# S4 convolution and MLP on one core: the outer products of the small tables as four operations, and a new order for everything ahead of the MLP

## The chip, the cores and the metric

The kernel runs on one core of one Trainium2 chip. Its time is device microseconds from one launch, and the median of three runs stands for it. The five engines are named as the profile names them: PE multiplies matrices, DVE and ACT do element-wise work, POOL is GpSimd, SP issues transfers. POOL issues transfers too. Each engine takes its instructions strictly in the order in which the program lists them, so an instruction that waits holds up everything behind it on its engine.

## What is computed

One layer with 2048 samples of 512 channels: a state-space convolution (S4) and an MLP, each behind two layer norms in a row. Cut to what matters:

```python
def _A_ref(u, A_re, A_im, B_re, B_im, C_re, C_im, log_dt, Dskip):
    dt = jnp.exp(log_dt)[:, None]
    logdA = dt * (A_re + 1j * A_im)                  # [D=512, N=128]
    P = jnp.exp(logdA[:, :, None] * l[None, None, :])  # l = 0..2047
    K = jnp.einsum("dn,dnl,dn->dl", Cc, P, dt * Bc).real
    y = irfft(rfft(pad(u)) * rfft(pad(K)))[:L]       # long convolution
    return y + u * Dskip
def _B_ref(x, w1, b1, w2, b2):
    h = _gelu(jnp.einsum("bsd,df->bsf", _layernorm(x), w1) + b1)   # F=1376
    return jnp.einsum("bsf,fd->bsd", h, w2) + b2
h  = x + _A_ref(_layernorm(x), ...)
h2 = h + _B_ref(_layernorm(h), ...)
```

## The kernel before

The work runs in two parts: a front, in which the convolution is made, and the MLP (`mlp`), which follows it. The channels are taken in two halves of 256.

**What the front does, stage by stage.** `params` turns the six parameter arrays into angles and logarithms of magnitudes, each split into pieces of bfloat16 that are then transposed by DMA (`TL`, `PL`, `QL`). `norm_in` makes the statistics of the input norm from `x`, some on ACT (`by_act`), the others on DVE (`bn_stats`), and ends in `roots`. `tables` makes the matrices of the Fourier transform (`M`, `Mn`, and turned `R`, `Rn`), partly from spread rows `Dp`. `outer` makes four small tables by outer products, `EP`, `EQ`, `RP` and `RQ`, which are the right-hand sides of later matmuls. `exps` then makes the magnitudes of powers of the state (PE into `ev`, ACT exponentials into `Pt` and `Q`); `p_half` and `q_half` make their phases (PE into `pv` and `qv`, ACT sines into `s` and `sq`, DVE products into `Pt` and `Q`). `kgen` multiplies the two (1024 small matmuls into `kps`, 128 to a step, four steps to each half of the channels) to the samples of the convolution kernel, the "second half's samples" being those of channels 256 to 511. They go to DRAM (`KD_near`, `KD_far`) and come back rearranged as `kt`. The normed input goes through PE (`aps`, `a`) to DRAM (`A_dram`) and comes back as `X`.

`conv` works one half of the channels at a time, in eight blocks `k2`: a spectrum of the kernel samples (`kfps`, 20 matmuls), its evacuation as `kf` (in the second half a real part on DVE, where the constant `tf` is added, and an imaginary part on ACT or DVE), a complex product with the spectrum of the input (`pa`, `pb` on DVE), the way back (`zps`, `z`), and the turn through DRAM (`Zd`, `ZT`). `x_stage` makes the spectrum of the input (`xps`, 8 matmuls per block). `early_rows` and `first_rows` make the first rows `y` for the MLP.

**How the order is made.** Each step is recorded as an operation with `S.op(engine, cost, ...)` and its dependencies. A step with a tuple of engines may stand on either. Nothing is decided while the kernel runs: the list `ORDER` holds one number per step, twice the step's index, plus one for the second engine of the tuple, and `Sched.run` emits the steps in that order. Buffers that rotate are handed out in that order too: three in PSUM with the tag "p", shared by `ev`, `aps`, `pv`, `qv`, `kps`, `xps`, `kfps` and the tables. An order across engines is kept by semaphores.

**Names that the change and the prediction touch.** The outer products stand in `outer`, as two operations on POOL, `make_e` and `make`, and `K.o_oute` and `K.o_out` are what `exps`, `p_half` and `q_half` wait for. Inner broadcasts make them:

```python
def wide(out, w, k, d):
    g.tensor_tensor(..., bc(w.unsqueeze(2), [P, k, d]), bc(m[...].unsqueeze(1), [P, k, d]), ALU.mult)
```

Bulk loads inside the front are the halves of the first MLP weight (`load_w1`, 384 KB each, `w`) and two blocks of the residual input (`residual`, 512 KB each, `X<-in_A_u_dram`). `put` and `get` in `kgen` are the transfers of the kernel samples.

Of the kernel before, what the change touches and what calls it, by code (L numbers as in the profile page):

```python
# [11 lines left out]
ALU = mybir.AluOpType  # L12
# [4 lines left out]
P = 128  # L17
# [14 lines left out]
AT = {"log": 1, "m0": 3, "m1": 3, "bases": 3, "sin0": 3, "exp": (1, 1), "sin": (3, 3)}  # L32
SETS = {1: "natural_log_exp_and_others", 3: "trig_and_small"}
ORDER = [
# [22 lines left out]
]  # L57


# [22 lines left out]
def bc(ap, shape):  # L82
    return ap.to_broadcast(shape)
# [199 lines left out]
def outer(nc, S, K, pp, c2):  # L283
# [7 lines left out]
    m, we = flat[:, 640:704], flat[:, 704:756]  # L291
    wp, wq = (flat[:, a:b].rearrange("p (i c) -> p i c", c=2) for a, b in ((768, 800), (800, 840)))
    g = nc.gpsimd
# [19 lines left out]
            count(nc, wq[p0:p1, at:at + cnt], base, pattern + [[0, 2]])  # L313
    pl = S.at(12.3)

    def wide(out, w, k, d):
        g.tensor_tensor(out[:].rearrange("p i c d -> p (i c) d") if len(out.shape) == 4 else out, bc(w.unsqueeze(2), [P, k, d]), bc(m[:, 0:32].unsqueeze(1) if d == 32 else m[:, 32:48].unsqueeze(1), [P, k, d]), ALU.mult)

    def make_e():
        g.tensor_tensor(m, K.ident[:, 0:64], K.ident[:, 64:128], ALU.add)  # L320
        g.tensor_tensor(m[:, 0:32], m[:, 0:32], m[:, 32:64], ALU.add)
        wide(K.EP, we[:, 0:32], 32, 32)
        wide(K.EQ[:, 0:20], we[:, 32:52], 20, 32)

    def make():
        g.tensor_tensor(m[:, 32:48], m[:, 0:16], m[:, 16:32], ALU.add)
        wide(K.RP, wp.rearrange("p i c -> p (i c)"), 32, 32)
        wide(K.RQ, wq.rearrange("p i c -> p (i c)"), 40, 16)

    K.o_oute = S.op("POOL", 4.0, make_e, [pl])  # L330
    K.o_out = S.op("POOL", 3.6, make, [K.o_oute])


def first_stage(nc, S, K, cp, c2, psp, dram):
# [330 lines left out]
def exps(nc, S, K, big, psp, hh, gate):  # L665
# [7 lines left out]
    for out, w, n, grp in ((K.o_pe, K.EP, 32, "pe"), (K.o_qe, K.EQ, 20, "qe")):  # L673
        S.group = f"{grp}{hh}"
        for b in range(8):
# [10 lines left out]
                o = K.Pt if grp == "pe" else K.Q  # L686
                nc.scalar.activation(o[:, :, 1, dq], cell["v"][:, 0:32 * n].rearrange("p (k d) -> p k d", d=32), ACT.Exp)  # L687

            x = S.op("PE", 0.45, ex, [K.o_tl[2 * hh + b // 4], K.o_oute, K.o_get], acq="p")
            K.o_ex[grp].append(x)  # L690
            out.append(S.op("ACT", 0.95, amp, [x, K.o_get], rel=[x], fun=AT["exp"][hh]))

# [34 lines left out]
def q_half(nc, S, K, sc, psp, hh):  # L727
    K.o_q, K.o_qp = [[], []], [[], []]
    for qd in range(2):
        S.group = f"q{hh}"  # L730
        for g in range(5):
            cell = {}
            b = 16 * hh + 8 * qd
# [16 lines left out]
                tt(nc, o, cell["s"][:], bc(o[:, :, 1:2, :], [P, m1 - m0, 2, nd]), ALU.mult)  # L750

            qe = K.o_qe[4 * qd + g:4 * qd + g + 1] if g < 4 else K.o_qe[4 * qd:4 * qd + 4]
            x = S.op("PE", 0.9, ph, K.o_ql[hh][2 * qd:2 * qd + 2] + [K.o_out] + qe, acq="p")
            K.o_qp[qd].append(x)
            z = S.op("ACT", 0.94, sn, [x], acq="s", rel=[x], fun=AT["sin"][hh])
            K.o_q[qd].append(S.op("DVE", 0.63, mul, [z] + qe, rel=[z]))
# [593 lines left out]
def kernel(ctx, tc, A_u, A_A_re, A_A_im, A_B_re, A_B_im, A_C_re, A_C_im, A_log_dt, A_Dskip,  # L1350
# [64 lines left out]
    part("x0", x_stage, psp, 0)  # L1415
    part("x1", x_stage, psp, 1)
    part("exps1", exps, big, psp, 1, K.o_kgen)
    done = None
    for n, ends in zip((3, 4, 5, 0, 1, 2), held + [K.o_ex["pe"], K.o_ex["qe"], K.o_ex["pe"] + K.o_ex["qe"]]):
# [79 lines left out]
```

## Time and profile before

| | us |
|---|---|
| three runs | 277.79, 280.06, 280.11 |
| median | 280.06 |
| the profiled execution, its own time | 279.49 |
| its span in the trace | 277.7 |
| PE busy | 246.3 (89%) |
| DVE busy | 208.4 (75%) |
| ACT busy | 170.7 (61%) |
| POOL busy | 51.4 (18%) |

The span leaves 1.79 us of that execution's time outside it. A stage table of the trace has one row per stretch of time: its start and end, its length, then busy microseconds and number of instructions of PE, of PE's weight loads, of DVE, ACT and POOL, then the granted clock of PE as a share of full speed, the mean busy share of the DMA engines, and the GB/s that they moved. A row of the timeline has the start, the duration, the engine, the line, the operation, what it wrote and read, its shape, how many instructions are merged in it, and in brackets the idle time of the engine before it and what ended that time. Stretches used here: up to 9.7 us loads and parameters, to 45 the statistics and tables, to 80 the first half's samples, to 97 the second half's exponentials, to 138 the second half's phases and samples together with the first half's convolution, to 152.6 the wait for the second half's samples, filled with other matmuls, to 189 the second half's convolution, and then the MLP.

### The profile page before, as it was taken

Reading aid. Unit: us, or ns where it says so; the run is one execution under the profiler, and the core shown is the slowest. Engines: PE = TensorE matmul, PEld = TensorE weight load, DVE = VectorE, ACT = ScalarE, POOL = GpSimd, SP = SyncE. Lnnn points to the kernel's source line nnn. Section 1 sums busy time; section 2 is a strip of 40 time slices with the busy share of each in tenths; the row PEclk is TensorE's granted clock in tenths of the full one; section 3 lists DMA queues with packets and bytes.
Section 4 is the critical chain, followed back from the end, with each engine's and each line's share of the span. In section 5 each row is a group of like instructions: output and inputs, shape, how many; then the busy total and the mean of one; then the engine's idle time right before and its main releaser. Section 6 shows DMA issues by size and latency. Waiting matters only on the chain.

```text
span 277.7 us, 6118 instructions
## 1 busy us (share of the span) xinstructions
PE 246.3 (89%) x2421; PEld 156.0 (56%) x2421; DVE 208.4 (75%) x447; ACT 170.7 (61%) x244; POOL 51.4 (18%) x121
## 2 busy tenths in 40 slices
PE   3647988788988899999799999889999999999995
PEld 2412333235743467888688887777874544544443
DVE  5799999999897577989588869878992883772012
ACT  5679999999769987683117346446880540630710
POOL 9992001950013300000033430201000000000000
PEclk9855559999977999999979999999999999999999
DMA  5700125997866269700449567767934104114001
GB/s 171 265 0 2 39 56 82 208 258 154 110 194 170 83 205 298 235 2 5 118 105 230 160 185 234 223 196 231 277 80 107 47 17 96 40 24 109 21 21 57
DMA packets 56737, 35.52 MB, mean 128 GB/s; under 512 B 29162, under 2 KB 55156, under 8 KB 56452
## 3 DMA queue, kind: packets, MB, share of 16 engines
q1 hardware_dynamic: 54884, 30.61, 42.7%
q0 software_dynamic: 1824, 4.51, 6.3%
q8 instruction: 19, 0.31, 0.4%
q14 instruction: 10, 0.08, 0.1%
HBM read 18.65 MB, written 11.21 MB: 108 GB/s over the span
## 4 chain that ended last, share of the span: by engine, by line
PE 57%; DVE 30%; ACT 6%; issue 4%; DMA 2%; SPq 1%; DVEq 0%; ACTq 0%
PE o2ps L1299 13%; PE h1ps L1287 12%; PE kfps L996 8%; PE kps L772 5%; DVE pa L79 3%; DVE Pt L79 3%; DVE a L91 3%; PE y L1104 2%; DVE w L79 2%; DVE st L851 2%; DVE w L121 2%; PE ev L683 2%; DVE Q L79 2%; PE aps L867 1%; DVE pb L79 1%
## 5 line engine op out<-in xcount | busy, mean ns | idle before, releaser
L1289 ACT ACTIVATE hT<-h1ps,b_sb 128x512 bf16<-128x512 f32 (+3 forms) x55 | 31.9, 611 | 36.8 <-PE h1ps L1287 36.8
L1287 PE MATMUL h1ps<-y2T,w 128*128 128x512 bf16 (+3 forms) x220 | 40.2, 336 | 0.5 <-DVE y2T L91 0.5
L1299 PE MATMUL o2ps<-w_sb,hT 128*128 128x512 bf16 (+3 forms) x187 | 38.7, 366 | 0.0
L996 PE MATMUL kfps<-kt,M 128*128 128x256 bf16 x320 | 38.6, 273 | 0.0
L79 DVE TENSOR_TENSOR ot<-o2ps,h 128x512 bf16<-128x512 f32 (+1 forms) x17 | 11.1, 659 | 31.3 <-PE o2ps L1299 19.8
L996 PEld LDWEIGHTS <-M 128*128 128x128 bf16 x320 | 31.5, 98 | 5.1 <-issue 0.9
L1287 PEld LDWEIGHTS <-w 128*128 128x128 bf16 (+1 forms) x220 | 21.9, 100 | 15.2 <-issue 0.6
L1299 PEld LDWEIGHTS <-hT 128*128 128x128 bf16 (+1 forms) x187 | 18.2, 98 | 19.7
L127 ACT ACTIVATE sq<-qv 128x1024 bf16<-128x1024 int16 x20 | 19.9, 1042 | 2.3 <-PE qv L742 2.0
L772 PEld LDWEIGHTS <-Pt 128*32 128x32 bf16 x1024 | 18.0, 169 | 5.9 <-issue 3.5
L772 PE MATMUL kps<-Q,Pt 128*32 128x20 bf16 x1024 | 19.0, 221 | 2.5 <-issue 2.0
L79 DVE TENSOR_TENSOR Pt<-s,Pt 128x1024 bf16<-128x1024 bf16 x32 | 20.5, 690 | 0.7 <-ACT s L127 0.7
L89 ACT CAST kf<-kfps 128x512 bf16<-128x512 f32 (+2 forms) x13 | 9.5, 739 | 14.4 <-DVE kf L79 9.3
L127 ACT ACTIVATE s<-pv 128x1024 bf16<-128x1024 int16 x16 | 15.9, 1027 | 2.8 <-issue 1.4
L687 ACT ACTIVATE Pt<-ev 128x1024 bf16<-128x1024 f32 x16 | 15.8, 1025 | 1.5 <-PE ev L683 1.3
L470 POOL DMA_DIRECT2D Dp<-Dd x24 | 12.2, 514 | 22.9 <-DVE u L862 21.8
L91 DVE CAST a<-aps 128x1024 bf16<-128x1024 f32 x11 | 13.4, 1223 | 2.3 <-PE aps L867 2.3
L683 PEld LDWEIGHTS <-TL 128*128 128x128 bf16 x64 | 7.1, 117 | 13.6 <-issue 10.3
L79 DVE TENSOR_TENSOR Q<-sq,Q 128x1024 bf16<-128x1024 bf16 x20 | 13.4, 689 | 0.7 <-ACT sq L127 0.6
L801 POOL DMA_DIRECT2D KD_far<-far x2 | 1.6, 797 | 64.5 <-DVE far L121 64.5
L89 ACT CAST X<-xps 128x1024 bf16<-128x1024 f32 x9 | 8.8, 1019 | 6.9 <-PE xps L908 6.9
L79 DVE TENSOR_TENSOR pa<-pa,pb 128x512 bf16<-128x512 bf16 (+1 forms) x34 | 12.4, 406 | 0.6
(247 smaller groups left out, 508.7 us busy)
## 6 DMA issues: line engine op xcount, KB each, us to landing
A_dram<-a SPq DMA_DIRECT2D x16, 256.0 KB, 3.3
X<-A_dram SPq DMA_DIRECT2D x4, 1024.0 KB, 6.5
Zd<-z SPq DMA_DIRECT2D x14, 256.0 KB, 2.6
ZT<-Zd SPq DMA_DIRECT2D x9, 256.0 KB, 4.2
x<-in_A_u_dram SPq DMA_DIRECT2D x4, 512.0 KB, 7.5
X<-in_A_u_dram SPq DMA_DIRECT2D x4, 512.0 KB, 9.5
out_dram<-ot SPq DMA_DIRECT2D x15, 128.0 KB, 1.7
ZT<-Zd POOLq DMA_DIRECT2D x7, 256.0 KB, 4.1
```

Source lines behind the costliest of these rows:

```text
L79: nc.vector.tensor_tensor(out, a, b, op)
L89: nc.scalar.copy(out, in_)
L91: nc.vector.tensor_copy(out, in_)
L127: nc.scalar.activation(out, v.bitcast(i16)[..., 0:2 * n:2], ACT.Sin, scale=S2PI / 65536)
L470: nc.gpsimd.dma_start(t[o::128 // cnt], bass.AP(row.tensor, row.offset + 1024 * kh, [[0, cnt], [1, 1024]]))
L683: nc.tensor.matmul(v[:, 32 * k:32 * k1], lhsT=K.TL[hh][:, b, :], rhs=w[:, k:k1].rearrange("p k d -> p (k d)"), start=True, stop=True)
L687: nc.scalar.activation(o[:, :, 1, dq], cell["v"][:, 0:32 * n].rearrange("p (k d) -> p k d", d=32), ACT.Exp)
L772: nc.tensor.matmul(kps[32 * g:32 * g + 32, i // 8, at:at + 20], lhsT=Pt[:, :, u, c], rhs=Q[:, :, u, c], start=True, stop=True, tile_positi ...
L996: nc.tensor.matmul(at, lhsT=K.M[:, t, 2 * k2 + k, c, :], rhs=kt[:, t, :], start=(c == 1 or hh == 1) and t == 0, stop=(t == 4))
L1287: nc.tensor.matmul(pt[:fs, 0:n], lhsT=K.w1_sb[:, dc, fc * P:fc * P + fs], rhs=y2T[tb][:, dc, js, :].rearrange("p a b -> p (a b)"), start=( ...
L1289: nc.scalar.activation(hT[tb % 2][:fs, fc, cols], pt[:fs, 0:n], ACT.Gelu_apprx_tanh, bias=K.b1_sb[:fs, fc:fc + 1], scale=1.0)
L1299: nc.tensor.matmul(pt[:], lhsT=h[:fs, fc, jj * P:(jj + 1) * P], rhs=K.w2_sb[:fs, fc, d], start=(fc == 0), stop=(fc == NFC - 1))
```

## The change

`outer` no longer has two operations but five: one for the small mask, on POOL, and one each for `EP`, `EQ`, `RP` and `RQ`, which may stand on DVE or POOL. What waited for both tables of a pair now waits for its own: `exps` for `EP` or `EQ`, `p_half` for `RP`, `q_half` for `RQ`. `ORDER` is a new list of all 711 steps. It puts `RP` on DVE, right behind `roots`, and the three other tables on POOL.

```diff
-    def make_e():
-        g.tensor_tensor(m, K.ident[:, 0:64], K.ident[:, 64:128], ALU.add)
-        ...
-        wide(K.EP, we[:, 0:32], 32, 32)
-        wide(K.EQ[:, 0:20], we[:, 32:52], 20, 32)
-    def make():
-        ...
-        wide(K.RP, wp.rearrange("p i c -> p (i c)"), 32, 32)
-        wide(K.RQ, wq.rearrange("p i c -> p (i c)"), 40, 16)
-    K.o_oute = S.op("POOL", 4.0, make_e, [pl])
-    K.o_out = S.op("POOL", 3.6, make, [K.o_oute])
+    def times(e, out, a, b, op):
+        (g if e == "POOL" else nc.vector).tensor_tensor(out, a, b, op)
+    ...
+    either = ("DVE", "POOL")
+    o_mask = S.op("POOL", 0.8, lambda: mask("POOL"), [pl])
+    K.o_oute = [S.op(either, (1.2, 1.9), lambda e: wide(e, K.EP, ...), [o_mask]),
+                S.op(either, (0.8, 1.2), lambda e: wide(e, K.EQ[:, 0:20], ...), [o_mask])]
+    K.o_out = S.op(either, (1.2, 1.9), lambda e: wide(e, K.RP, ...), [o_mask])
+    K.o_outq = S.op(either, (0.8, 1.2), lambda e: wide(e, K.RQ, ...), [o_mask])
@@ exps
-            x = S.op("PE", 0.45, ex, [K.o_tl[2 * hh + b // 4], K.o_oute, K.o_get], acq="p")
+            x = S.op("PE", 0.45, ex, [K.o_tl[2 * hh + b // 4], K.o_oute[grp == "qe"], K.o_get], acq="p")
@@ q_half
-            x = S.op("PE", 0.9, ph, K.o_ql[hh][2 * qd:2 * qd + 2] + [K.o_out] + qe, acq="p")
+            x = S.op("PE", 0.9, ph, K.o_ql[hh][2 * qd:2 * qd + 2] + [K.o_outq] + qe, acq="p")
@@ ORDER
-    368, 60, 66, 0, 86, 2, 54, 364, ...
+    60, 204, 68, 0, 64, 72, 74, 66, ...
```

What the new list does, read out of it step by step:

- ACT's first sine (`wb`) stands behind the first table of sines, so the first table load of sines at the start falls away; the front has six table loads, not seven.
- On DVE, `freq` (`nf`, `nn`) stands right behind the first product of the parameters; the lower piece of that product stands later. `RP` stands behind `roots`, `last_row` after the first evacuation of `aps`.
- On PE, `cim` is turned ahead of `bre`.
- The scaling of `M` block 1 stands on ACT. Of the evacuations of `aps`, `xps`, `zps` and `kfps` about as many go from DVE to ACT as the other way.
- Ahead of the last `kgen` matmuls of the second half PE has four more blocks (three `xps`, one `zps`) and one `kfps` less; DVE has one more product of the first half (`k2` = 7) ahead of the end of `kgen`. Before the first `kfps` of the second half PE has one more `xps` and one more `zps`.
- The imaginary parts of blocks `k2` = 0 and 5 of the second half stand on DVE.
- Both residual blocks are issued by POOL, behind the last `get` of the second half's samples on POOL; before, the first was issued by SP ahead of the second half's puts. The first half of the weight `w` goes to SP, behind the put of `KD_far` and ahead of three of the five gets; the second to POOL, behind the one get there. The put of `KD_far` goes from POOL to SP and stands behind the first get there, which waits for `KD_near`.
- The bias load of the MLP on POOL stands behind the first half's gets.

More of the change, by code (lines that the diff above doesn't have):

```diff
@@ L314, in outer, with wide, mask @@
     pl = S.at(12.3)
-    def wide(out, w, k, d):
-        g.tensor_tensor(out[:].rearrange("p i c d -> p (i c) d") if len(out.shape) == 4 else out, bc(w.unsqueeze(2), [P, k, d]), bc(m[:, 0:32].unsqueeze(1) if d == 32 else m[:, 32:48].unsqueeze(1), [P, k, d]), ALU.mult)
-    def make_e():
-        g.tensor_tensor(m, K.ident[:, 0:64], K.ident[:, 64:128], ALU.add)
-        g.tensor_tensor(m[:, 0:32], m[:, 0:32], m[:, 32:64], ALU.add)
-        wide(K.EP, we[:, 0:32], 32, 32)
-        wide(K.EQ[:, 0:20], we[:, 32:52], 20, 32)
-    def make():
-        g.tensor_tensor(m[:, 32:48], m[:, 0:16], m[:, 16:32], ALU.add)
-        wide(K.RP, wp.rearrange("p i c -> p (i c)"), 32, 32)
-        wide(K.RQ, wq.rearrange("p i c -> p (i c)"), 40, 16)
-    K.o_oute = S.op("POOL", 4.0, make_e, [pl])
-    K.o_out = S.op("POOL", 3.6, make, [K.o_oute])
+    def times(e, out, a, b, op):
+        (g if e == "POOL" else nc.vector).tensor_tensor(out, a, b, op)
+    def wide(e, out, w, k, d):
+        times(e, out[:].rearrange("p i c d -> p (i c) d") if len(out.shape) == 4 else out, bc(w.unsqueeze(2), [P, k, d]), bc(m[:, 0:32].unsqueeze(1) if d == 32 else m[:, 32:48].unsqueeze(1), [P, k, d]), ALU.mult)
+    def mask(e):
+        times(e, m, K.ident[:, 0:64], K.ident[:, 64:128], ALU.add)
+        times(e, m[:, 0:32], m[:, 0:32], m[:, 32:64], ALU.add)
+        times(e, m[:, 32:48], m[:, 0:16], m[:, 16:32], ALU.add)
+    either = ("DVE", "POOL")
+    o_mask = S.op("POOL", 0.8, lambda: mask("POOL"), [pl])
+    K.o_oute = [S.op(either, (1.2, 1.9), lambda e: wide(e, K.EP, we[:, 0:32], 32, 32), [o_mask]),
+                S.op(either, (0.8, 1.2), lambda e: wide(e, K.EQ[:, 0:20], we[:, 32:52], 20, 32), [o_mask])]
+    K.o_out = S.op(either, (1.2, 1.9), lambda e: wide(e, K.RP, wp.rearrange("p i c -> p (i c)"), 32, 32), [o_mask])
+    K.o_outq = S.op(either, (0.8, 1.2), lambda e: wide(e, K.RQ, wq.rearrange("p i c -> p (i c)"), 40, 16), [o_mask])
 def first_stage(nc, S, K, cp, c2, psp, dram):
```

44 rows, old and new, of the table ORDER are left out of this document.

## Prediction

> **What bounds the kernel now.** I read the stage table first, because the mean shares of the page mix stages with different limits.
>
> ```profile
> 9.70:45.00 35.30, 26.33 (x77) 9.23 (x78) 34.20 (x81) 32.77 (x59) 12.26 (x22) 0.56 0.25 54
> 45.00:80.00 35.00, 29.27 (x605) 16.62 (x604) 33.57 (x61) 31.41 (x36) 12.17 (x24) 1.00 0.86 177
> 80.00:97.00 17.00, 14.24 (x60) 6.02 (x58) 12.05 (x18) 15.55 (x20) 5.41 (x8) 0.80 0.49 134
> 97.00:138.00 41.00, 38.87 (x756) 31.73 (x754) 34.14 (x55) 24.33 (x27) 0.00 (x0) 1.00 0.52 146
> 138.00:152.60 14.60, 14.60 (x120) 12.38 (x119) 11.98 (x17) 6.50 (x8) 4.50 (x7) 0.88 0.66 158
> 152.60:189.00 36.40, 33.60 (x304) 29.39 (x302) 30.00 (x60) 17.11 (x22) 7.14 (x8) 1.00 0.71 204
> 189.00:277.70 88.70, 84.75 (x487) 46.91 (x485) 48.01 (x136) 37.84 (x69) 1.17 (x3) 1.00 0.31 83
> ```
>
> Up to 80 us DVE is the bound (34.20 of 35.30, 33.57 of 35.00), with ACT close behind. From 80 to 97 it is ACT (15.55 of 17.00). From 97 on it is PE: 38.87 of 41.00, then no idle at all, then 33.60 of 36.40. The last 88.7 us are the MLP, whose code the change leaves alone; it only starts earlier or later. So moving work between engines pays up to 80 us only if DVE gets less of it, and after 97 only where PE idles or runs slowly.
>
> The timeline of DVE and POOL shows what POOL's outer products do to DVE.
>
> ```profile
> 9.66 1.29 DVE L79 TENSOR_TENSOR w<-tps_bre,w 128x512 f32<-128x512 f32 x2 [1.83 <-ACT w L89]
> 10.98 0.69 DVE L79 TENSOR_TENSOR w<-w,w 128x512 f32<-128x512 f32 x1
> 12.66 1.90 POOL L317 TENSOR_TENSOR EP<-EQ 128x1024 bf16<-128x1024 bf16 x1
> 12.90 2.21 DVE L79 TENSOR_TENSOR w<-w,w 128x512 f32<-128x512 f32 x1
> 16.37 1.89 POOL L317 TENSOR_TENSOR RP<-EQ 128x1024 bf16<-128x1024 bf16 x1
> 16.77 2.04 DVE L121 SCALAR_TENSOR_TENSOR w<-w,w 128x512 f32<-128x512 f32 x1
> 20.59 0.67 DVE L121 SCALAR_TENSOR_TENSOR w<-w 128x512 f32<-128x512 f32 x1
> ```
>
> The same DVE product takes 0.69 us alone and 2.21 us beside `EP`; the one beside `RP` takes 2.04 us where 0.67 us is its price later. Each time DVE ends about 0.55 us after POOL: one waits for the other.
>
> **The change part by part.** *The outer products and the front (to 80 us).* `RP` leaves POOL, so one lock falls away: 2.04 - 0.67 = 1.37 us of DVE. The other three stay and go on holding DVE. `RP` itself comes to DVE behind `roots`, where DVE has no idle time to hide it. No row shows it on DVE.
>
> ```profile
> L79 DVE TENSOR_TENSOR Pt<-s,Pt 128x1024 bf16<-128x1024 bf16 x32 | 20.5, 690 | 0.7 <-ACT s L127 0.7
> 27.61 0.50 DVE L79 TENSOR_TENSOR nf<-lf,fs 128x336 f32<-128x336 f32 x1
> 28.14 0.58 DVE L73 TENSOR_SCALAR nn<-nf 128x336 int32<-128x336 f32 x2
> 28.75 0.51 DVE L73 TENSOR_SCALAR nn<-nn 128x672 int32<-128x672 int32 x1
> 7.16 0.67 DVE L79 TENSOR_TENSOR M<-w,M 128x512 bf16<-128x512 f32 x1
> 159.25 0.69 DVE L79 TENSOR_TENSOR kf<-kfps,tf 128x512 bf16<-128x512 f32 x1 [1.14 <-ACT kf L89]
> ```
>
> A product of the same size takes 0.69 us, the lower bound; POOL's 1.89 us is the upper. The row most like it is `nf`, which also broadcasts along the innermost axis: 0.50 x 1024 / 336 = 1.52 us with its fixed part counted three times, so I take 1.3. `freq` (`nf` and `nn`, 0.50 + 0.58 + 0.51 = 1.6 us) moves into the 1.83 us in which DVE waits before 9.66, and the 0.67 us piece comes out of cover: -0.9 us. DVE's own sum is then 1.3 - 1.4 - 0.9 = -1.0 us. Against it stand new waits: seven times in the front a DVE step needs an ACT step that needs a DVE step (the first cast of `psi`, its second piece, the cast of `psw`, the logarithm's cast, the arctangent, its piece, the sine for `dirichlet`), and the new lists stand closer together at several of them. A crossing left uncovered costs 1.14 us on the row that shows one alone (159.25, from the second half's convolution). Followed through both lists, the arctangent, the second `psi` piece and half the first cast come out late, so I take +1.6 and the front as +0.6 us; bounds -1.0 (all covered) and +7.6 (seven at 1.14, `RP` at 1.89). One table load less at the start hides nothing: its successor waits for parameters that land at about the same time. `cim` ahead of `bre` only makes room for `freq`.
>
> *The second half's exponentials (80 to 97).* DVE loses the scaling of `M` there and the `aps` that hold PSUM buffers stand later among the exponentials.
>
> ```profile
> 83.27 1.02 ACT L687 ACTIVATE Pt<-ev 128x1024 bf16<-128x1024 f32 x1 [0.88 <-PE ev L683]
> 87.45 2.85 ACT L687 ACTIVATE Pt<-ev 128x1024 bf16<-128x1024 f32 x3 [0.44 <-PE ev L683]
> ```
>
> ACT, the bound, idles 0.88 + 0.44 = 1.32 us here for PE. The new order starts with four short exponentials behind a single `aps`. I take -1.0 us, bounds 0 and -1.32. The scaling of `M`, now on ACT, stands among the `kps` of the first half, where ACT waits for PE; without that cover its 2048 elements cost twice the 1.02 us of a 1024-element row.
>
> *The residual load ahead of the second half's samples.*
>
> ```profile
> 131.78 0.45 SPq L1196 DMA_DIRECT2D X<-in_A_u_dram  x1
> 133.81 2.02 PE L772 MATMUL kps<-Q,Pt 128*32 128x20 bf16 x109
> 137.50 0.45 PE L772 MATMUL kps<-Q,Pt 128*32 128x20 bf16 x15 [1.67 <-issue]
> 138.40:141.30 2.90, 2.90 (x16) 2.01 (x14) 1.97 (x4) 0.36 (x1) 0.79 (x1) 0.50 0.23 75
> 143.99 0.11 PE xps L906
> q1 hardware_dynamic: 281, 0.14, 48.5%
> q8 instruction: 1, 0.02, 5.6%
> ```
>
> In the midst of its last `kps` block PE stands still for 1.67 us, waiting for nothing that the profile names. The transfer queues between 135 and 136 us (last two rows) hold the end of the residual load, issued at 131.78, and one packet of instructions. That PE's instructions queued behind the load is my reading, not a row. From 138.4 to 141.3 the granted clock is 0.50, so that stretch lost 2.90 x 0.5 = 1.45 us; at full clock an `xps` matmul takes 0.11 us. The new order issues this load from POOL behind the `get`s. I take both as gone: -1.67 and -1.45 us, each with 0 as its other bound. [...]
>
> PE's work before the end of `kgen` grows by four blocks of 8 matmuls and shrinks by 20 matmuls, at 0.11 us: (32 - 20) x 0.11 = 1.3 us later; 16 more stand between there and the second half's first `kfps`, and those 20. All of it leaves later stretches that PE bounds too, so it cancels.
>
> *The second half's convolution (152.6 to 189).*
>
> ```profile
> 152.56 4.53 PE L996 MATMUL kfps<-kt,M 128*128 128x256 bf16 x40
> 157.43 0.68 DVE L79 TENSOR_TENSOR kf<-kfps,tf 128x512 bf16<-128x512 f32 x1
> 159.86 0.68 DVE L79 TENSOR_TENSOR pa<-X,kf 128x1024 bf16<-128x1024 bf16 x1
> 160.46 0.69 DVE L79 TENSOR_TENSOR pb<-X,kf 128x1024 bf16<-128x1024 bf16 x1
> 161.18 0.76 DVE L79 TENSOR_TENSOR pa<-pa,pb 128x512 bf16<-128x512 bf16 x2
> 166.65 0.69 DVE L79 TENSOR_TENSOR kf<-kfps,tf 128x512 bf16<-128x512 f32 x1 [2.11 <-ACT kf L89]
> ```
>
> PE has the first block by about 154.8 (half of 4.53 us in), but DVE, still at products of the first half, takes it up at 157.43, and the first product of the second half starts at 159.86. Later DVE waits 1.14 us (159.25) and 2.11 us for ACT's imaginary parts. PE stands 36.40 - 33.60 = 2.80 us in all. The change puts one first-half product (159.86 to 161.85, 2.0 us) ahead of the end of `kgen`, and the imaginary part of the first block on DVE, which ends the crossing there. The backlog then fits into the wait for the samples and PE becomes the bound from the first block. I take -2.0 us of the 2.80; bounds 0 and -2.8.
>
> *The sum.* The profiled execution took 279.49 us, 0.57 below the median of 280.06: 279.49 + 0.6 - 1.0 - 1.67 - 1.45 - 2.0 = 273.97, so 274.0 us.
>
> **The rivals.** *The stall stays.* The blocks of `kgen` stand as close as before (one `zps` between the last two), and instruction packets may run short without any load beside them. For: the load's packets end in the row of 135 to 136 us, the stall only at 137.5. Against: the other three blocks of that half, issued before this load moved data, show no such gap. 274.0 + 1.67 + 1.45 = 277.1 us.
>
> *The second half's samples come back late.*
>
> ```profile
> 139.18 0.33 SPq L803 DMA_DIRECT2D KD_near<-near  x1
> 139.77 0.79 POOL L801 DMA_DIRECT2D KD_far<-far  x1 [42.77 <-DVE far L121]
> 140.89 0.36 SPq L809 DMA_DIRECT2D kt<-KD_near  x1
> 142.62 0.78 POOL L809 DMA_DIRECT2D kt<-KD_far  x1 [2.06 <-DMA KD_far<-far]
> w<-in_B_w_dram POOLq DMA_DIRECT2D x1, 384.0 KB, 7.3
> ```
>
> The put of `KD_far` now stands on SP behind a `get` that waits for `KD_near`, 140.89 - 139.18 = 1.7 us after its put: it starts 2.1 us after the near put instead of 0.6. Behind it on SP come two small transfers and half of `w`, then three of the five `get`s, for which every `kfps` of that half waits. `w` would start at about 3.3 and land at 10.6 us after the near put; the `get`s, if they land only behind it with 2.85 us of their own (what far's put took, 139.77 to 142.62) and a second such for the queue, at 16.3. PE needs them at 152.6 - 139.2 = 13.4, less 1.45 for the restored clock, plus 0.4 for what moves into the gap ((20 + 16 - 32) x 0.11): 12.4. That is 3.9 us of waiting, 277.9 us. Against it: transfers of this size overlapped in this stretch before.
>
> *The front slips (slower).* DVE takes its steps in order, so each ACT step that comes late stops it, and ACT then starts its 16 exponentials late too. Place: 18 to 46 us. Price: at the upper bound +7.6 in place of +0.6: 281.0 us. It decides from the sixth uncovered crossing (0.6 + 6.1 us over the forecast). For: DVE and ACT were both nearly without idle there, and POOL's three locks stay. Against: both lists keep distance at four of seven.
>
> **How the numbers follow.** Forecast 0.50; the stall stays 0.14; late samples 0.16; the front slips 0.20. All gains in full give 279.49 - 1.0 - 1.32 - 1.67 - 1.45 - 2.8 = 271.25, the low end at 271.0; the high end is the slip, 281.0. A measurement here can tell about 1% from no change: under 277.3 and over 282.9 us. Faster takes the forecast and 0.05 of the staying stall, 0.55; slower takes 0.15 of the slip (its crossings can cost more than 1.14) and 0.03 of the late samples, 0.18; the rest, 0.27, lies within.
>
> **What would show it.** Right: no DVE product near 2 us beside `RP`, which takes 1.3 us on DVE around 45; the first half's samples done at about 80 as before; no gap in the last `kps` and a clock near 1.0 behind it; the first second-half product within 4 us of its first `kfps`; PE idle under 1 us to the MLP. Wrong: DVE gaps behind ACT between 18 and 46, or a `kfps` released by a `kt` transfer.

## The result and the profile after

| | before | after |
|---|---|---|
| median of 20 runs each | 280.1 us (276.16 to 281.9) | 275.9 us (273.64 to 279.68) |
| ratio after/before | | 0.9888, 95% interval 0.9858 to 0.9918 |

The changed kernel is 1.1% faster; 274.0 us was forecast. Measured twice more, beside the experiments, its ratio was 0.9816 (0.9766 to 0.9866) and 0.9772 (0.9707 to 0.9837). A ratio leaves disturbed runs out on both sides (in the group of `after_res`, 12 of the 17 runs of the kernel before), so it need not be the ratio of the medians beside it.

The profile read here is that of a second measurement (`after_again`): 272.38 us for that execution, span 270.6 us. In the first one, of 278.16 us, PE's clock was at half in three places between 46 us and the MLP, here in none; the last section comes back to this. Three rows of the stage table after, in the columns of the one before:

```profile
80.00:97.00 17.00, 14.39 (x81) 7.40 (x83) 12.46 (x19) 16.73 (x22) 5.55 (x10) 1.00 0.82 182
138.00:152.60 14.60, 14.60 (x136) 13.08 (x135) 11.71 (x20) 6.16 (x7) 6.58 (x10) 1.00 0.96 244
152.60:189.00 36.40, 32.85 (x297) 28.30 (x295) 29.36 (x66) 19.64 (x30) 7.51 (x10) 1.00 0.72 199
```

Two things strike the eye: the clock of 138 to 152.6 went from 0.88 to 1.00, and in that same stretch the transfer engines are now busy 0.96 of the time, where it was 0.66. A table by fixed times mixes stages that have moved, so I went on by milestones: rows that both kernels have, at the end of each stage. First before, then after; the table loads of ACT open the first half's sines, the second half's exponentials and its sines, `near` ends `kgen`, the `kf` is the first real part of the second half, and `st<-y` is the first statistic of a whole row.

```profile
49.59 1.28 ACT L161 ACT_TABLE_LOAD   x1
80.07 1.28 ACT L161 ACT_TABLE_LOAD   x1
95.56 1.28 ACT L161 ACT_TABLE_LOAD   x1
138.80 0.35 DVE L121 SCALAR_TENSOR_TENSOR near<-kps,half_sign,ku 128x128 bf16<-128x128 f32 x1 [2.73 <-ACT ku L776]
190.96 0.76 DVE L1254 BATCH_NORM_STATS2 st<-y 128x6 f32<-128x256 f32 x2 [0.84 <-PE y L1151]
```

```profile
47.73 1.28 ACT L161 ACT_TABLE_LOAD   x1
78.06 1.28 ACT L161 ACT_TABLE_LOAD   x1
92.07 1.28 ACT L161 ACT_TABLE_LOAD   x1
133.97 0.35 DVE L121 SCALAR_TENSOR_TENSOR near<-kps,half_sign,ku 128x128 bf16<-128x128 f32 x1 [2.65 <-ACT ku L777]
149.99 0.68 DVE L79 TENSOR_TENSOR kf<-kfps,tf 128x512 bf16<-128x512 f32 x1
183.84 0.76 DVE L1255 BATCH_NORM_STATS2 st<-y 128x6 f32<-128x256 f32 x2 [2.73 <-PE y L1152]
```

| from one milestone to the next | before | after | difference | forecast |
|---|---|---|---|---|
| start to the first sines | 49.59 | 47.73 | -1.86 | +0.6 |
| to the second half's exponentials | 30.48 | 30.33 | -0.15 | 0 |
| to its sines | 15.49 | 14.01 | -1.48 | -1.0 |
| to the end of `kgen` | 43.24 | 41.90 | -1.34 | -1.67 |
| to the first real part of the second half (before: 157.43) | 18.63 | 16.02 | -2.61 | -1.45 (the clock), and with the next row |
| to the whole rows | 33.53 | 33.85 | +0.32 | -2.0 (the convolution) |
| to the end of the span | 86.74 | 86.76 | +0.02 | 0 |

The sum is -7.1 us, which is what separates these two executions (279.49 and 272.38), not the medians. Forecast was -5.5. Where the last stages lost is in the rows around 156 us: three of the four bulk loads that SP and POOL had issued before (the other half of `w` at 141.41), then ACT's `z` and PE's next matmul behind it.

```profile
138.62 0.38 SPq L1171 DMA_DIRECT2D w<-in_B_w_dram  x1
142.16 0.93 POOL L1197 DMA_DIRECT2D X<-in_A_u_dram  x1
143.66 0.93 POOL L1197 DMA_DIRECT2D X<-in_A_u_dram  x1
155.59 1.01 ACT L89 CAST z<-zps 128x1024 bf16<-128x1024 f32 x1 [1.58 <-DMA Zd<-z]
156.66 0.27 PE L1039 MATMUL zps<-pa,R 128*128 128x256 bf16 x1 [2.07 <-ACT z L89]
```

ACT cannot take the next `z` because the buffer's old contents are not yet written to DRAM. In the list of transfers a write of `Zd` takes 8.1 us from issue to landing (median of 14), where it took 2.6 us before. PE stands 2.07 us for it. This wait was no step of the forecast.

### The profile page after: what moved, and what is told of

The parts are those of the page before. It is cut to its first block, busy times and chain, and to the rows that moved or that the text cites. A ratio compares the mean times of both kernels' runs of the same rounds, so it can differ in the third digit from the quotient of the medians.

```text
span 276.4 us, 6123 instructions
## 1 busy us (share of the span) xinstructions
PE 248.9 (90%) x2421; PEld 156.4 (57%) x2421; DVE 205.3 (74%) x446; ACT 171.7 (62%) x245; POOL 49.7 (18%) x120
## 4 chain that ended last, share of the span: by engine, by line
PE 59%; ACT 19%; DMA 10%; DVE 8%; issue 2%; SPq 1%; DVEq 0%; ACTq 0%
PE o2ps L1300 13%; PE h1ps L1288 13%; PE kfps L997 10%; DMA Zd<-z 6%; PE kps L773 5%; ACT Pt L688 5%; DVE Pt L79 3%; PE ev L684 3%; DMA x<-in_A_u_dram 2%; PE qv L743 2%; ACT L161 2%; ACT Q L688 2%; PE y L1105 2%; DVE Q L79 1%; ACT u L850 1%
## 5 line engine op out<-in xcount | busy, mean ns | idle before, releaser
L997 PE MATMUL kfps<-kt,M 128*128 128x256 bf16 x320 | 40.1, 280 | 0.0
L89 ACT CAST kf<-kfps 128x512 bf16<-128x512 f32 (+2 forms) x11 | 7.8, 705 | 13.8 <-DVE kf L79 6.4
L89 ACT CAST X<-xps 128x1024 bf16<-128x1024 f32 x12 | 12.3, 1022 | 6.0 <-PE xps L909 6.0
L89 ACT CAST z<-zps 128x1024 bf16<-128x1024 f32 x10 | 10.2, 1016 | 5.9 <-PE zps L1042 3.9
L743 PE MATMUL qv<-RQ,QL 128*128 128x128 bf16 (+1 forms) x64 | 12.1, 306 | 1.6 <-ACT sq L127 0.9
```

Of the source, the lines that this page charges most:

```text
L89: nc.scalar.copy(out, in_)
L743: nc.tensor.matmul(v[:, n], lhsT=K.QL[(b + n) // 8][:, (b + n) % 8, :], rhs=K.RQ[:, m0:m1].rearrange("p i c d -> p (i c d)"), start=True, ...
L997: nc.tensor.matmul(at, lhsT=K.M[:, t, 2 * k2 + k, c, :], rhs=kt[:, t, :], start=(c == 1 or hh == 1) and t == 0, stop=(t == 4))
```

## The experiments

Twelve measurements in three groups of four, each group on one chip together with runs of the kernel before. Where a kernel is built with another order list, its lines stand four lower in the file (L313 for L317). A splice takes all steps up to one step from one list and the rest from the other.

### Is the wait for `z` the kernel's own? (`after_again`)

No edit.

> The changed kernel once more, for a profile in which the clock is not disturbed. In its first profile ACT's evacuation z at 159.53 waits 1.90 us for a write Zd<-z that was issued at 148.34 and took 11.10 us; PE then stands 2.39 us up to 160.60, and its clock is 0.61 and 0.50 from 161.5 to 165.3. If this is the kernel's own, the same wait of PE, 2 to 3 us, and the same low clock behind it stand in this profile too. If it came from the disturbance, z waits for no write here. Time 275.9 us in both cases (0.985 of before).

275.75 us (272.38 to 276.81, 6 runs; before 280.33 us), ratio 0.9816. The wait is there: 1.58 us of ACT and 2.07 us of PE, rows above. The clock behind it stays at 1.00, so the slow stretch that stood behind the wait in the first profile is not a fixed part of it. `after_ref`, below, has the wait too: PE stands 2.45 us there.

### The first residual load alone, in the kernel before (`before_res`)

```diff
 SP:  write z0[4:6]
-     residual[0]
      put near, get, ... second half of w
+     residual[0]
```

> The kernel before with one step moved: the first residual block (512 KB), issued by SP at 131.78 us ahead of the second half's samples, now stands on SP behind the second half of w, at about 165 us. Theory: the load holds back PE's instructions, so the gap of 1.67 us in the last kps block goes, and with it the slow clock from 138.4 to 141.3 (1.45 us): 280.1 - 3.1 = 277.0 us. Rival one: the instruction packet is late without a load beside it: 280.1 us, the gap stays. Rival two: the gap goes and the low clock has another cause: 280.1 - 1.7 = 278.4 us.

278.56 us (276.38 to 280.32, 12 runs), ratio 0.9923 (0.9891 to 0.9954), which is 1.3 to 3.1 us of 280.33; the medians are 1.8 us apart. The timeline of PE in the last `kps` block, and a row of the stage table:

```profile
133.51 2.11 PE L768 MATMUL kps<-Q,Pt 128*32 128x20 bf16 x113
135.97 0.46 PE L768 MATMUL kps<-Q,Pt 128*32 128x20 bf16 x15 [0.35 <-issue]
138.00:152.60 14.60, 14.60 (x136) 13.08 (x134) 14.22 (x20) 7.07 (x8) 4.50 (x7) 1.00 0.81 209
```

The block breaks at the same place, behind 113 matmuls, but for 0.35 us instead of 1.67, and the clock behind it is 1.00 instead of 0.88. Its profiled execution (276.38 us) is 3.1 us below that of before, as the theory says, but it is the fastest of the twelve; the median lies next to rival two (278.4 us). That the load makes the gap is shown, and rival one is out. The slow clock went with the gap in this execution; that the gap makes it is not shown (see the clock, below).

### The outer products alone, in the kernel before (`before_rp`)

```diff
 POOL: mask, EP, EQ, 
-      RP, RQ
+      RQ
 DVE:  ... roots
+      RP
```

> The kernel before with the outer products alone changed: four operations, EP, EQ and RQ on POOL in the old order, RP on DVE right behind roots; the rest of the order as before. Theory (the prediction's): one lock less, 1.37 us, and RP on DVE at 1.2 us (it took 1.22 in the changed kernel): 279.9 us, no difference that can be told. Rival one: the time won before roots lasts, because ACT's exponentials start 1.4 us earlier and RP is done beside their head: 278.7 us. Rival two: RP behind roots holds up the DVE products on which PE waits, and the lock is only passed on to the next DVE operation: 281.3 us.

280.97 us (280.07 to 282.83, 12 runs), ratio 1.0034 (1.0004 to 1.0063): no gain, if anything a loss of under 1.8 us. Rows of DVE, ACT and PE:

```profile
13.27 2.01 DVE L75 TENSOR_TENSOR w<-w,w 128x512 f32<-128x512 f32 x1
44.06 1.22 DVE L313 TENSOR_TENSOR RP<-EQ 128x1024 bf16<-128x1024 bf16 x1
50.07 1.28 ACT L157 ACT_TABLE_LOAD   x1
139.56 0.45 PE L769 MATMUL kps<-Q,Pt 128*32 128x20 bf16 x15 [1.99 <-issue]
```

DVE is held at `EP` as before (2.01 us) and twice more behind it (1.00 us for `st<-tot` at 15.44, 1.22 us for the product at 16.95), then pays 1.22 us for `RP`, and the sines begin at 50.07, 0.48 us later than before. The theory (no difference) is nearly right, rival two in direction. The gap in `kps` stays, 1.99 us. The execution profiled is the longest of the twelve (282.83 us), and its clock is at 0.50 for much of the time from 74 to 146 us, behind these sines.

### All bulk loads later (`after_bulk`)

```diff
 SP:  ... turn z0[4]
+     residual[0], residual[1]
      ... write z1[4:6]
+     first half of w
      ... write z1[8:10]
+     second half of w
 POOL/SP behind the gets:
-     both halves of w, residual[0], residual[1]
```

> The changed kernel with its four bulk loads issued later on SP: both residual blocks behind the turns of the first half's convolution, both halves of w among the writes of the second half's. Theory: the loads between 142 and 148 us (1.8 MB) are what makes the write of z take 11 us, so PE's 2.39 us and the slow clock behind it (2.0 x 0.39 + 1.8 x 0.50 = 1.7 us) go: 275.9 - 4.1 = 271.8 us. Rival one: the write is late because of the other writes and turns of its own queue; then nothing changes, 275.9 us. Rival two: the loads now delay the second half's writes and turns, or the residual comes late for the first rows, and what is won is given back: 274 to 277 us.

277.0 us (274.76 to 279.3, 6 runs), ratio 0.9857 (0.9808 to 0.9906): not 271.8. Rows of ACT and PE:

```profile
170.44 1.01 ACT L85 CAST z<-zps 128x1024 bf16<-128x1024 f32 x1 [5.18 <-DMA Zd<-z]
171.50 0.27 PE L1035 MATMUL zps<-pa,R 128*128 128x256 bf16 x1 [2.06 <-ACT z L85]
187.33 1.07 PE L1143 MATMUL y<-ZT,Dm 96*128 96x256 bf16 x8 [3.25 <-DMA ZT<-Zd]
```

The gap at 157 us is gone, and with the loads it went to 171 us; a turn is late for 3.25 us at the end too. Rival two held. The loads do make the wait, but moving all four only moves it. (The rows are of its longest execution, 279.30 us, the only one profiled.)

### Only the first residual load, early (`after_res`)

```diff
 SP:  ... Dg[6]
+     residual[0]
      put near, ...
 POOL behind the gets:
-     residual[0]
```

> The changed kernel (275.8 us) with its first residual block (512 KB) back on SP ahead of the second half's puts; SP reaches it at about 121 us. Theory: what made PE wait in the kernel before is a packet of instructions that is fetched while the load moves; at 121 to 125 us a fetch can meet it too, then a gap of 1.5 us or more stands in PE there and the clock may fall behind it: 277 to 279 us. Rival one: the load is through before the fetch for the last kps block, no gap returns, and with 512 KB less between 138 and 150 us z's wait for its write, and PE's 2.1 us behind it, shrink: 273.8 us. Rival two: no gap, but z waits as before for the 1.3 MB that stay there: 275.8 us.

274.25 us (272.27 to 276.82, 6 runs; before 281.1 us), ratio 0.9839 (0.9739 to 0.994). Rows of SP and PE, and the writes of `Zd` between 140 and 165 us, of this kernel and then of `after_again`:

```profile
123.00 0.38 SPq L1193 DMA_DIRECT2D X<-in_A_u_dram  x1
132.44 2.33 PE L769 MATMUL kps<-Q,Pt 128*32 128x20 bf16 x128
156.33 0.27 PE L1035 MATMUL zps<-pa,R 128*128 128x256 bf16 x1 [0.40 <-ACT z L85]
Zd<-z SPq DMA_DIRECT2D x8, 256.0 KB, 5.3
```

```profile
Zd<-z SPq DMA_DIRECT2D x8, 256.0 KB, 8.1
```

Issued 8.8 us earlier than in the kernel before, the same load on the same queue opens no gap in any `kps` block. With 512 KB less in the crowded stretch a write of `Zd` takes 5.3 instead of 8.1 us, and PE waits 0.40 instead of 2.07 us. Rival one (273.8 us) held. By the profiles, from the end of `kgen` (135.33) to the whole rows (183.81) it takes 48.48 us, `after_again` 49.87 and `before_res` (137.26 to 187.87) 50.61. In time it can't be told from the changed kernel: the intervals overlap.

### The same, and one half of `w` later (`after_mix`, `after_mix2`)

```diff
 (as after_res)
 SP:  ... turn z0[4]
+     second half of w
 POOL behind the gets:
-     second half of w
```

> As after_res, and the second half of w (384 KB) issued by SP behind the turns of the first half's convolution, at about 158 us, so that 0.9 MB of bulk loads stay between 138 and 150 us, as much as in the kernel before. Theory: PE's gap of 2.1 us in front of 157 us goes and no new one comes: 273.7 us. Rival one: as in after_bulk the wait only moves to a later write of z, about 170 us, or to a turn: 275 to 277 us. Rival two: the early residual load stops PE at 121 to 125 us: 277 us.

272.69 us (271.16 to 276.57, 7 runs; before 281.1 us), ratio 0.9815 (0.9744 to 0.9887). Since this looked like the best version, it was run again beside the changed kernel.

> The same kernel as after_mix, again, beside the changed kernel on one chip: the first residual block early, at about 121 us, and the second half of w late, at about 158 us. Theory: 3.1 us less than the changed kernel, as in the first measurement (272.7 against 275.8), of which PE's wait of 2.1 us for z is one part, and z waits for no write in its profile. Rival: the difference between the chips of the two calls made it, and the two are alike within 1 us here.

273.76 us (272.16 to 276.63, 6 runs) against 276.01 us (272.25 to 278.67) of the changed kernel on the same chip; ratios to before 0.9742 (0.9695 to 0.979) and 0.9772 (0.9707 to 0.9837). The medians are 2.25 us apart, but the intervals overlap: that it beats the changed kernel is likely, not shown. A row of PE:

```profile
181.56 1.03 PE L1143 MATMUL y<-ZT,Dm 96*128 96x256 bf16 x8 [1.68 <-DMA ZT<-Zd]
```

PE's wait for `z` is down to 0.40 us, but a turn is 1.68 us late at the end (0.52 us in `after_res`, which differs in nothing but this half of `w`), so that of the 1.7 us won most is given back: from the end of `kgen` (134.07) to the whole rows (183.72) 49.65 us, 0.2 less than in `after_again`. As in `after_bulk`, a later `w` is paid for at the last turns.

### The lists spliced (`ab_roots`, `ba_roots`, `ab_k1x`)

```diff
 ab_roots: new list up to roots,                the rest in the old order
 ba_roots: old list up to roots,                the rest in the new order
 ab_k1x:   new list up to the last near, far,   the rest in the old order,
           residual[0] behind the second half of w
```

> Order spliced: the changed kernel's list up to roots (42.6 us), all other steps in the order of the kernel before (280.2 us), its residual load ahead of the second half's puts too; RP stands on POOL's or DVE's place as the old order has it (POOL). Theory: DVE ends roots 2.1 us earlier (44.70 to 42.6) and all behind it is as before, so the gain lasts: 278.1 us. Rival one: ACT's exponentials and sines bound the stretch to 80 us, and the gain is lost there: 280.2 us. Rival two: what is left for behind roots (lower pieces, casts) crowds DVE there: 281 us.

279.79 us (279.11 to 282.8, 12 runs; before 281.1 us, 276.19 to 283.98), ratio 1.0075 (1.0027 to 1.0124). The medians say a little faster, the ratio a little slower; neither shows the 2 us of the theory. Rows of ACT and PE:

```profile
48.54 1.28 ACT L157 ACT_TABLE_LOAD   x1
137.48 0.45 PE L769 MATMUL kps<-Q,Pt 128*32 128x20 bf16 x15 [2.50 <-issue]
```

The sines begin 1.05 us earlier, those of the second half, at 94.69, still 0.87 us earlier, and the gap in `kps`, which this kernel keeps, is 0.83 us longer than in the profile of before: it takes back what was won. The slow clock there lasts 6.8 us, against 3.4 us before.

> Order spliced the other way: the list of the kernel before up to roots, with all four outer products on POOL, and all other steps in the order of the changed kernel. Theory: the new front is worth the 1.9 us by which ACT's first sines begin earlier (49.59 to 47.73), and behind it nothing gives them back: 275.8 + 1.9 = 277.7 us. Rival: the steps up to 80 us are bound by PE and ACT behind roots, and the new front is worth nothing in the end: 275.8 us.

281.76 us (279.56 to 286.82, 12 runs; before 280.7 us), ratio 1.0027 (0.9998 to 1.0056). Both theories missed by 4 us and more. Rows of ACT and PE:

```profile
49.80 1.28 ACT L157 ACT_TABLE_LOAD   x1
56.10 0.99 PE L739 MATMUL qv<-RQ,QL 128*128 128x128 bf16 x5 [2.92 <-DMA QL<-M]
83.94 1.28 ACT L157 ACT_TABLE_LOAD   x1
```

The sines take 34.14 us here, 30.33 in `after_again`: PE waits 2.92 us for a turned piece of `QL`, which this mixture issues too late, and the clock is at 0.50 for 3.4 us from 56.2 on. So the new rest needs the new front not for its end at `roots` but for what it has issued by then; a splice here measures the seam as well.

> Order spliced: the changed kernel's list up to the last evacuation of kps (kgen's end), all other steps in the order of the kernel before, but its first residual block late, behind the second half of w (as in before_res). Theory: the second half's convolution in the new order is worth nothing any more, because z's wait for its write gives back what the earlier first product won; then this kernel takes what the changed one takes, 275.8 us, or less by the PE gap of 2.1 us that it doesn't have: 273.7 us. Rival: the new order of the second half is worth the 2.0 us of the forecast even so: 277.8 us.

274.89 us (273.12 to 277.88, 6 runs; before 281.1 us), ratio 0.9888 (0.9797 to 0.9979). Rows of DVE:

```profile
152.85 0.69 DVE L75 TENSOR_TENSOR kf<-kfps,tf 128x512 bf16<-128x512 f32 x1 [1.14 <-ACT kf L85]
184.67 0.76 DVE L1251 BATCH_NORM_STATS2 st<-y 128x6 f32<-128x256 f32 x2 [0.92 <-PE y L1148]
```

With the old order behind `kgen` and its load out of the way, the kernel takes what the changed one takes, as the theory has it, though the interval of the ratio does not exclude the rival. From the end of `kgen` (134.14) to the whole rows it needs 50.53 us against 49.87, with DVE's old wait of 1.14 us in it. The new second half's convolution, with the loads in its way, is worth 0.7 us in the profiles; no difference in time is measured.

### `RP` back on POOL, in the changed kernel (`after_rp`, `after_ref`)

```diff
 POOL: mask, EP, EQ,
-      RQ
+      RP, RQ
 DVE:  ... roots
-      RP
```

> The changed kernel with RP back on POOL, between EQ and RQ; all else in the new order. Theory: DVE is rid of RP's 1.22 us behind roots and pays with one more lock, about 1.4 us beside RP at 17 to 19 us; ACT's sines begin at 47.7 us as in the changed kernel or up to 0.3 us earlier or later: 275.8 us, the same as the changed kernel. Rival one: RP on DVE is what won the front; then the sines begin 1.9 us later and the time goes to 277.7 us. Rival two: the new order keeps DVE clear of POOL here too, no lock, and DVE is 1.22 us ahead: 274.6 us.

> The changed kernel itself on the chip of the three others, to compare them with: 275.8 us, 0.984 of before; z waits 1.6 to 1.9 us for its write and PE 2.1 to 2.4 us behind it, near 157 us.

277.18 us (273.93 to 279.51, 6 runs) against 276.01 us (272.25 to 278.67, 6 runs) of the changed kernel: ratios 0.9857 (0.9798 to 0.9916) and 0.9772 (0.9707 to 0.9837), not told apart for certain. Rows of DVE and ACT, while POOL has `EQ` from 15.54, `RP` from 16.76 and `RQ` from 19.14:

```profile
15.58 1.25 DVE L69 TENSOR_SCALAR st<-tot 128x12 f32<-128x12 f32 x1 [1.33 <-ACT u L844]
18.89 2.10 DVE L117 SCALAR_TENSOR_TENSOR w<-w,M 128x128 f32<-128x128 f32 x4 [0.22 <-ACT w L608]
48.80 1.28 ACT L157 ACT_TABLE_LOAD   x1
```

A lock comes back, as expected (2.10 us for what takes 0.90 in `after_again`). The one of about 1.1 us on `st`, beside `EQ`, does not come from `RP`: in `before_rp`, with `RP` on DVE, the same step took 1.00 us at 15.44, beside `EQ` too. The sines begin 1.07 us later than in `after_again`, between the theory (within 0.3) and rival one (1.9), but only 0.08 us later than in `after_ref` (48.72). In all eight profiles with the new front and `RP` on DVE they begin at 47.73 to 48.72, with `RP` on POOL at 48.54 (`ab_roots`) and 48.80. So in the new order `RP` on DVE is worth about 1 us at best by the profiles; in the old order (`before_rp`) nothing. The reason can be read from ACT. From its second table load to the sines it takes 13.53 us in `after_again` and in `after_rp` (34.20 to 47.73, 35.27 to 48.80): in the new order the 1.22 us of `RP` on DVE do not delay it. In the old order they do: 13.85 us before, 14.98 us in `before_rp`.

## Why the prediction was right, and where it was not

**The front: wrong in sign, +0.6 forecast, -1.86 measured.** Two steps failed. The first is "The other three stay and go on holding DVE". The start of DVE and POOL after:

```profile
12.72 0.73 DVE L79 TENSOR_TENSOR w<-w,w 128x512 f32<-128x512 f32 x1
13.37 0.68 DVE L852 BATCH_NORM_STATS2 st<-x 128x6 f32<-128x512 bf16 x1
15.32 0.18 DVE L73 TENSOR_SCALAR st<-tot 128x12 f32<-128x12 f32 x1 [1.26 <-ACT u L848]
15.84 1.32 DVE L121 SCALAR_TENSOR_TENSOR w<-w,w 128x512 f32<-128x512 f32 x1 [0.34 <-ACT w L609]
13.49 1.90 POOL L317 TENSOR_TENSOR EP<-EQ 128x1024 bf16<-128x1024 bf16 x1
16.57 1.70 POOL L317 TENSOR_TENSOR RQ<-EQ 128x640 bf16<-128x640 bf16 x1
42.58 1.22 DVE L317 TENSOR_TENSOR RP<-EQ 128x1024 bf16<-128x1024 bf16 x1
```

The product that took 2.21 us before takes 0.73: it gets in before `EP` begins, and while `EP` runs DVE does statistics of `x` and waits for ACT. One lock is left, at 15.84, of 1.32 - 0.67 = 0.65 us. Before there were 2.21 - 0.69 and 2.04 - 0.67 in the rows of the prediction, and a third that it did not list, beside `EQ` (14.52 to 16.23):

```profile
15.04 1.23 DVE L73 TENSOR_SCALAR st<-tot 128x12 f32<-128x12 f32 x1
```

The same step takes 0.18 us at 15.32 in the rows after, so this lock was 1.05 us. In all 3.9 us of locks became 0.65: 3.3 us went, not 1.37. `RP` itself cost 1.22 us, 1.3 forecast. The second is the +1.6 us for uncovered crossings: waits of 1.26 + 0.34 = 1.6 us came, but at 15 us, in time that the locks took before; between 18 and 46 us DVE shows one, of 0.15 us. The forecast judged the crossings by the list and the locks by the trace; both had to be followed through the new list in time. How much the front gains differs between executions: in the eight profiles with the new front and `RP` on DVE the sines begin 0.87 to 1.86 us earlier than before.

**The second half's exponentials: -1.0 forecast, -1.48 measured.** The size is about right, the reason was not. The granted clock between these two table loads was 0.78 before and is 1.00 here. In five profiles with the new order and the clock at 1.00 there (`after_again`, `after_mix2`, `ab_k1x`, `after_rp`, `after_ref`) the stage takes 14.0 us; in five with the new order and 0.89 to 0.92 (`after`, `after_bulk`, `after_mix`, `after_res`, `ba_roots`), 14.95 to 15.22. `before_res`, with the old order and 0.90, takes 14.92. At a like clock the new order gains nothing, so the record speaks for the clock: the forecast took ACT's waits for PE for a matter of the order. `after_res`, with the new order, has 1.6 us of such waits. That the size fits is luck.

**The residual load: right.** -1.67 us forecast; -1.32 in `before_res` (95.34 to 137.26 is 41.92 us), which moves nothing else and keeps 0.35 us of the gap. The changed kernel's -1.34 is the same by chance: its gap is gone whole, but PE is busy 41.40 us in that stretch, 40.69 us in `before_res`. The gap stood in every kernel that kept the load at its old place (1.67, 1.99, 2.50 us), and in no other was it over 0.35 us. That PE's instructions are what the load holds back stays a reading.

**The clock: the gain came, the cause did not hold.** Its price in this stretch was 18.63 - 16.97 = 1.66 us (`before_res`, 137.26 to 154.23), 1.45 forecast. The step that failed is that the gap makes the slow stretch. A row of `before_rp`, from ahead of its gap, which opens at 137.57, and then two of `after_mix`, which has no gap:

```profile
135.60:137.50 1.90, 1.90 (x113) 1.87 (x112) 1.87 (x5) 0.00 (x0) 0.00 (x0) 0.50 0.81 215
```

```profile
133.60:137.00 3.40, 3.37 (x137) 2.97 (x136) 0.68 (x2) 1.27 (x2) 0.00 (x0) 1.00 0.02 5
137.00:140.40 3.40, 3.40 (x18) 2.37 (x17) 1.81 (x3) 0.07 (x1) 0.00 (x0) 0.50 0.39 116
```

In `before_rp` the clock fell 2 us before PE stood still; in `after_mix` it fell with PE busy 3.37 of the 3.40 us before. It was slow around the last `kps` in all three profiles with a gap of 1.67 us or more, and in one of the eleven others. So a gap may help, but the slow stretch is not its work alone, and that `after_again` has none is in part luck.

**The second half's convolution: the mechanism right, the sum wrong.** The first product came 3.7 us behind the first `kfps`, within the 4 us forecast, and DVE's wait of 1.14 us at the second block went. But from the end of `kgen` to the whole rows the changed kernel gains only 50.61 - 49.87 = 0.74 us over `before_res`, not 2.0. The step that failed is "PE becomes the bound from the first block": PE is idle 3.0 us there, 2.6 us in `before_res`, where under 1 us was the sign of being right. The forecast listed that four bulk loads now stand behind the `get`s and asked only whether `kt` comes late; it did not ask about the next transfer on whose landing a buffer depends, `Zd`. `after_res`, with one load less in the way, shows 50.61 - 48.48 = 2.13 us: that load took 1.4 us. But only 1.0 of the 2.13 is idle time of PE (2.6 us became 1.6). The other 1.1 is PE work (47.97 us became 46.85) that moved ahead of the end of `kgen`, where it cost nothing because PE idled less there (from 97 to 138 us 0.03 us, 1.20 in `before_res`).

**The rivals.** The stall did not stay. `kt` was not late: PE has no idle time from 138 to 152.6 us. The front did not slip. The slow stretch was missing at its place, but it can come without the gap. What was missing was a rival in which the loads, freed from one collision, run into another.

**From the profile to the median.** `after_again`'s profiled execution lies 3.4 us below its own median, that of before 0.6 below the 280.1. So the -7.1 us of the milestones is the best of the changed kernel against a usual run of the old one. `after_ref`, an execution of 275.22 us, shows what a usual run loses: its tables are loaded at 48.72, 80.94 and 94.93 us, 1.0 us more to the sines and 1.9 us more within them, the same behind. That the median came within 2 us of the forecast is in part luck: the front won where a loss was forecast, and the convolution and the clock of a usual run gave that back.

## What to carry to other kernels

A bulk load that is moved can take its price along: before moving it, list the transfers on which buffers and instructions depend in the stretch where it lands, not only the one it was moved away from. In `after_bulk` PE's 2.07 us at 157 us became 2.06 us at 171 us, and a turn was late for 3.25 us. The cheapest place found here, by the profiles, was one in which the transfer engines were nearly idle (busy 0.05 of the time from 122 to 127 us in `after_again`, which has no load there), 12.7 us ahead of the second half's puts (`after_res`), not behind them. And what splitting an operation is worth depends on the order around it: the same `RP` on DVE gave nothing in the old list and at best about 1 us in the new.

## What the runs showed of the hardware

**The clock differs between executions of one kernel.** A row of a table by stretches of `after_again`, then the same of `after_ref`, the same kernel; the column before the last two is the granted clock:

```profile
68.00:70.00 2.00, 1.95 (x50) 1.26 (x44) 2.00 (x6) 1.79 (x3) 0.00 (x0) 1.00 0.71 193
```

```profile
68.00:70.00 2.00, 2.00 (x128) 2.00 (x123) 2.00 (x4) 1.73 (x2) 0.00 (x0) 0.50 0.52 100
```

This accounts for the 1.9 us above: from the first sines to the second half's exponentials the kernels with the new list up to there take 30.1 to 30.4 us in the five profiles without a slow stretch between 60 and 75 us, 31.15 in `after_bulk` with 3.4 us of it, and 32.0 to 32.25 in three with 6.8 us.

**Slow stretches come in steps of 3.4 us.** The fourteen profiles have 21 slow stretches between 46 us and the whole rows. Thirteen last 3.4 us, six 6.8, one 10.25 and one 13.65. In the first profiles of both kernels their starts lie whole multiples of 3.41 us apart: 66.37, 80.02 and 161.94 us in the changed one (4 and 24 steps), 80.20 and 138.23 before (17). That the clock is set anew every 3.41 us is my reading of these starts and lengths. A gap is not enough: PE's 2.07 us at 156 us left the clock at 1.00, as did 2.45 us in `after_ref`, while 1.67 us in the kernel before did not. Nor is one needed (`after_mix`, above). What makes the clock fall is open; no run tests it.

**A full clock ahead of 45 us was worth nothing.** `before_res` ran that stretch at 1.00, before at 0.56:

```profile
9.70:45.00 35.30, 28.55 (x79) 10.10 (x79) 33.57 (x79) 33.05 (x59) 12.55 (x22) 1.00 0.25 54
```

Its sines began at 49.90 us, before at 49.59: PE does not bound that stage.

**Not every DVE operation is held by POOL.** In the rows of the front above, the statistics at 13.37 took 0.68 us with `EP` running beside them for most of that time (0.69 us at 21.97 before, with POOL done with its tables), and a product that reads PSUM (`psi<-tps_are`, 17.74, 0.67 us in the same profile) ran beside `RQ` at the length that its like, `w<-tps_are,M`, had at 6.18 (0.69 us), ahead of the tables. The products that took 2.0 to 2.2 us, 2.21 and 2.04 before and 2.01 in `before_rp`, have two operands in SBUF. A step with a single small operand was held too: `st<-tot`, 1.23 us beside `EQ` before. What decides which operation is held is not shown; no run tests it. The trace of the kernel before has operations that were not held, too: `psi<-tps_are` at 16.17 took 0.68 us beside `RP`, two statistics at 18.74 took 1.27 us beside `RQ`. From these the forecast could have asked, lock by lock, which DVE operation stands beside each table in the new list.
